# Threshold attention with a GELU layer behind it: early turns split in two, tail copies on another engine, weight conversion shifted between slots

## The chip, the cores and the metric

The kernel runs on one core of one Trainium2 chip. The core has a matrix engine (TensorE, "PE" in the profile, with its weight loads shown apart as "PEld"), a vector engine (VectorE, "DVE"), an activation engine (ScalarE, "ACT"), a general engine (GpSimd, "POOL"), and a queue engine that mostly starts transfers (SyncE, "SP"). They run side by side and wait for each other by semaphores. TensorE writes into PSUM, the small accumulation memory; the others work on SBUF, and VectorE and ScalarE read PSUM too.

The metric is device time in microseconds (us), the median of several runs. Lower is better.

## The reference

```python
scores = scale * np.matmul(q, k.transpose(0, 1, 3, 2))       # q, k, v: (8, 8, 576, 64), float32
thresh = np.max(scores, axis=-1, keepdims=True) - tau
scores = np.where(scores >= thresh, scores, -1000000000.0)
scores = scores - np.max(scores, axis=-1, keepdims=True)
attn = np.exp(scores)
attn = attn / (np.sum(attn, axis=-1, keepdims=True) + 1e-09)
out = np.matmul(attn, v)
x = out.transpose(0, 2, 1, 3).reshape(4608, 512)             # tokens x model
h = x @ w_in                                                 # w_in: (512, 2048)
g = 0.5 * h * (1.0 + erf(h / sqrt(2)))
return g @ w_out                                             # w_out: (2048, 512)
```

Attention per head, in which all keys that score less than the row's best minus tau are dropped, and behind it a two-layer network with an exact GELU. The two weight matrices reach the kernel as 64-bit floating-point numbers; it turns them into 32-bit ones itself.

## The kernel before

**Pairs and slots.** Heads are worked two at a time. There are 32 pairs, four to a batch (HP = 4); the first four (EARLY) are treated differently from the others. The 576 rows of a head are four chunks of 128 (MAIN = 512) and a tail of 64; the two tails of a pair share a fifth chunk. One chunk of one pair is a slot, one turn of the main loop at L1140, counted by `n` from 0. For the early pairs the order is: slots 0 to 7 are chunks 0 and 1 of pairs 0 to 3, slots 8 to 19 are chunks 2, 3 and 4 (the tails) of pairs 0 to 3. From slot 20 (BATCH) on a pair has its five slots in a row. All of the order is written out by hand in this loop; each engine works through its own instructions in the order of the program.

**What a slot does.** `scores` (L403) multiplies the chunk's q with all of k into two PSUM tiles tagged "sc", of which there are two. `softmax_head` takes the negated row maximum on VectorE (L415), the threshold on POOL (L418), and the exponential on ScalarE (L420). `softmax_tail` applies the threshold and sums the row on VectorE (L436); this also frees the "sc" tile for the next slot's scores. Every other PSUM tile has the tag "mm", of which there are four.

**Turning.** For the early pairs q and k are loaded row-wise and transposed by TensorE against the identity, in `turn_qk_early` (L299): 16 matmul records for q, 16 for k, then the tails; one copy of 512 columns for each (L320 for q with its scale, L322 for k, on VectorE for pair zero and on ScalarE for the others), two small copies for k's tail (L330, L331) and two for q's tail (L334). A slot's probabilities are transposed one slot later by `turn_p_early` (L347, nine records) and copied by ScalarE: two copies of 512 columns (L354) and one of 128, the tail columns (L362).

**Weighting.** Two slots after its own, a chunk is multiplied with v. For pairs 2 and 3 (HALVED) this is `weigh_half` for chunk 0 and then for chunk 1 (L606, 128 columns each); for pairs 0 and 1 both chunks together in `weigh_v` (L574, 256 columns), in the slot of the second. `divide_early` then spreads the reciprocals of the row sums over partitions (L493, L495) and POOL multiplies (L501). Chunks 2 to 4 are weighted together later and divided late by `divide_late`; their divisors go through memory on the SP queue (`divisors_early`, L460 to L468).

**Weight conversion.** The weights are 32 pieces (16 of w_in, then 16 of w_out). `load_piece` (L161) starts the transfer of the next raw piece on the SP queue, to one of the seven buffers `xall` or to a part of `turned_p`, and gives up if no buffer is free. A conversion step is two ScalarE activations of 512 columns (`convert_first`, L199, L200), two VectorE operations (`convert_second`, L207, L208), which then ask for another piece, and one POOL addition (L219) in the next slot. `STEPS[n]` says how many steps slot n does, at its end, behind its L436. ScalarE's part runs one piece ahead of VectorE's.

**The network in the early slots.** From slot 10 on `fill` puts the first layer of the first block of tokens between the attention work: some 6.4 matmuls (L674) a slot. Eight matmuls complete a tile hT; it is appended to `late` and copied out of PSUM by ScalarE (L641) when `gelus` is called with a smaller number than are waiting: `lag` inside the fill, 0 after the exponentials of every slot. `keep_busy` adds idle matmuls (L297) in slots 1, 6 and 8.

**Behind slot 20** the same loop goes on with other helpers; `lag` is set to 2 there, and `last_blocks` ends the kernel.

## Time and profile before

| what | value |
|---|---|
| median of 3 runs | 1329.47 us (1329.26 to 1331.39) |
| the profiled execution, its own time | 1329.71 us |
| its span, first to last instruction | 1327.70 us |
| TensorE busy | 1315.7 us, 99% |
| VectorE busy | 1040.3 us, 78% |
| ScalarE busy | 604.9 us, 46% |
| GpSimd busy | 637.1 us, 48% |
| first scores of slot 0 | 7.57 us |
| first scores of slot 10 | 57.21 us |
| first scores of slot 20 | 121.03 us |

The profile is of one execution. Its times count from the first instruction; the execution as timed from outside took 2.01 us more. A matmul of 32-bit numbers shows as two records. The end of a matmul is modelled, so a busy TensorE may hide short waits, for example inside a row of score records that is split in two because the second "sc" tile came free late. In a row of the timeline the brackets at the end give how long the engine stood idle and what it waited for. "In line" below means an operation right behind another on its engine, which starts before the shown end of the one in front of it; what it adds is less than its own duration.

### The profile page before, as it was taken

To read this page: it belongs to the slowest core of one execution; us is meant where nothing else is said; L and a number is where in the kernel's file an instruction comes from. 1 tells how busy PE (TensorE), PEld (TensorE's weight loads), DVE (VectorE), ACT (ScalarE), POOL (GpSimd) and SP (SyncE) were. 2 spreads that over 40 slices of the span, in tenths; PEclk is the share of its full clock that TensorE was granted. 3 is DMA by queue.
4 is the path that set the end of the run, shared out by engine and by line. 5 is a ranking of instruction groups with operands and counts; after the bars stand their busy time and mean duration, and the time that the engine had idled before them with its cause. 6 is when DMAs were issued, how large, how long until landed. Compare 5 with 4: busy or idle time off the path is not lost.

```text
span 1327.7 us, 19863 instructions
## 1 busy us (share of the span) xinstructions
PE 1315.7 (99%) x6306; PEld 889.1 (67%) x6306; DVE 1040.3 (78%) x2001; ACT 604.9 (46%) x1027; POOL 637.1 (48%) x1058
## 2 busy tenths in 40 slices
PE   9999999999999999999999999999999999999998
PEld 6776466576476466466466466578778787877877
DVE  6887877888888888888888888883857698386674
ACT  7988366376376368358458438232111203211120
POOL 3565545455555555655555541236264403645430
PEclk9999999999999999999999999999999999999999
DMA  7553667777776787787787775400000140000003
GB/s 250 180 177 89 143 156 164 168 161 161 190 167 157 191 185 160 191 194 164 185 202 159 177 172 110 105 9 1 1 0 1 40 107 14 0 1 0 1 0 80
DMA packets 213687, 153.14 MB, mean 115 GB/s; under 512 B 117264, under 2 KB 196992, under 8 KB 213584
## 3 DMA queue, kind: packets, MB, share of 16 engines
q1 hardware_dynamic: 195440, 125.31, 40.6%
q0 software_dynamic: 17712, 26.26, 7.4%
q8 instruction: 52, 0.85, 0.3%
q14 instruction: 51, 0.42, 0.1%
q10 hardware_dynamic: 432, 0.30, 0.1%
HBM read 56.62 MB, written 12.58 MB: 52 GB/s over the span
## 4 chain that ended last, share of the span: by engine, by line
PE 92%; ACT 2%; DVE 2%; DMA 1%; issue 1%; POOL 1%; SPq 0%; DVEq 0%; POOLq 0%; ACTq 0%
PE bank L862 34%; PE o_ps L689 17%; PE hT L674 16%; PE sc L403 13%; PE xT L574 11%; ACT p L420 1%; DVE nmx L415 1%; DMA inv<-turned 0%; PE tr L347 0%; ACT pT L354 0%; DVE p L436 0%; DVE power L208 0%; DVE power L207 0%; DMA xall<-in_moe_w_out_dram 0%; DMA turned_p<-in_moe_w_out_dram 0%
## 5 line engine op out<-in xcount | busy, mean ns | idle before, releaser
L420 ACT ACTIVATE p<-sc,nmx 128x576 f32<-128x576 f32 x288 | 202.0, 738 | 277.9 <-DVE nmx L415 277.6
L436 DVE SCALAR_TENSOR_TENSOR p<-sc,thr,p 128x576 f32<-128x576 f32 x288 | 225.4, 816 | 72.7 <-ACT p L420 65.2
L418 POOL TENSOR_SCALAR thr<-nmx,tau_eff 128x1 f32<-128x1 f32 x288 | 84.7, 296 | 335.1 <-DVE nmx L415 332.5
L674 PE MATMUL hT<-xall,w_in 128*128 128x256 f32 x1024 | 241.8, 385 | 0.0
L415 DVE TENSOR_REDUCE nmx<-sc 128x1 f32<-128x576 f32 x288 | 205.2, 749 | 44.3 <-PE sc L403 43.0
L689 PE MATMUL o_ps<-w_out,g 128*128 128x512 f32 x512 | 236.7, 602 | 0.0
L674 PEld LDWEIGHTS hT<-xall,w_in 128*128 128x128 f32 x1024 | 189.4, 190 | 51.3 <-issue 24.5
L744 DVE TENSOR_TENSOR o<-o,bank 128x256 f32<-128x256 f32 (+1 forms) x242 | 100.0, 417 | 94.5 <-PE bank L862 89.5
L744 DVE TENSOR_TENSOR c<-c,bank 128x320 f32<-128x320 f32 x304 | 146.7, 487 | 34.3 <-PE bank L862 21.1
L689 PEld LDWEIGHTS o_ps<-w_out,g 128*128 128x128 f32 x512 | 93.1, 190 | 109.6 <-issue 106.8
L403 PE MATMUL sc<-kT,qT 64*128 64x288 f32 x960 | 161.3, 429 | 2.1 <-DVE p L436 1.2
L574 PE MATMUL xT<-pT,v 128*64 128x320 f32 (+1 forms) x1240 | 159.3, 409 | 0.2
L535 DVE STREAM_TRANSPOSE turned_p<-p 128x1152 f32<-128x1152 f32 x112 | 154.4, 1378 | 3.9
L403 PEld LDWEIGHTS sc<-kT,qT 64*128 64x128 f32 x960 | 91.8, 186 | 77.0 <-issue 61.9
L574 PEld LDWEIGHTS xT<-pT,v 128*64 128x64 f32 x1240 | 86.4, 137 | 70.9 <-issue 10.4
L862 PE MATMUL bank<-w_out,c 128*128 128x256 f32 (+1 forms) x484 | 120.5, 379 | 0.8 <-DVE o L744 0.8
L260 POOL DMA_DIRECT2D v<-in_v_dram x208 | 111.2, 538 | 3.4 <-issue 1.2
L862 PEld LDWEIGHTS bank<-w_out,c 128*128 128x128 f32 x484 | 90.3, 190 | 18.9 <-DVE o L744 3.2
L929 ACT ACTIVATE c<-c 128x320 f32<-128x320 f32 (+1 forms) x80 | 46.9, 624 | 114.7 <-DVE c L744 114.6
L744 POOL TENSOR_TENSOR c<-c,g 128x320 f32<-128x320 f32 (+1 forms) x40 | 50.6, 1273 | 67.4 <-DVE c L744 67.4
L862 PE MATMUL bank<-t_out,g 128*128 128x256 f32 (+1 forms) x324 | 82.4, 377 | 0.4 <-DVE o L744 0.4
L862 PE MATMUL bank<-t_out,c 128*128 128x256 f32 x320 | 82.8, 381 | 0.0
(185 smaller groups left out, 1749.1 us busy)
## 6 DMA issues: line engine op xcount, KB each, us to landing
pT<-turned_p SPq DMA_DIRECT2D x448, 160.0 KB, 3.6
pT<-pd_tail SPq DMA_DIRECT2D x112, 80.0 KB, 3.0
q<-in_q_dram POOLq DMA_DIRECT2D x104, 72.0 KB, 3.6
k<-in_k_dram POOLq DMA_DIRECT2D x104, 72.0 KB, 3.2
inv<-turned SPq DMA_DIRECT2D x54, 128.0 KB, 4.0
v<-in_v_dram POOLq DMA_DIRECT2D x156, 40.0 KB, 3.1
out_dram<-o SPq DMA_DIRECT2D x40, 128.0 KB, 2.4
xall<-in_moe_w_out_dram SPq DMA_DIRECT2D x9, 512.0 KB, 4.9
```

Source lines behind the costliest of these rows:

```text
L260: eng.dma_start(t[r:P:4, e, 0:n, :], rows[:, r * KR:r * KR + n, :])
L403: nc.tensor.matmul(sc[e][:, h, 0:HALF], lhsT=lhsT, rhs=s["kT"][rows, at:at + HALF], start=True, stop=True)
L415: nc.vector.tensor_reduce(nmx[:, e:e + 1], sc, axis=AXIS.XY, op=ALU.max, negate=True)
L418: nc.gpsimd.tensor_scalar(thr[:, e:e + 1], nmx[:, e:e + 1], -1.0, tau_eff, op0=ALU.mult, op1=ALU.subtract)
L420: nc.scalar.activation(w[:, e * S:(e + 1) * S].rearrange("p (h s) -> p h s", h=2), sc, AF.Exp, bias=nmx[:, e:e + 1], scale=1.0)
L436: nc.vector.scalar_tensor_tensor(row, sc[e][:, :, 0:HALF], thr[:, e:e + 1], row, op0=ALU.is_ge, op1=ALU.mult, accum_out=den[e])
L535: nc.vector.transpose(turned_p[:, :, i // 2, 0:NB, i % 2 * Q:(i % 2 + 1) * Q], w.rearrange("p (e b i) -> p e b i", e=2, i=Q))
L574: nc.tensor.matmul(to, lhsT=s["v"][:, e, c, :], rhs=rhs, start=(c == 0), stop=(c == KR - 1))
L674: nc.tensor.matmul(hT[:, j % 2, :], lhsT=w_in_sb[c][:, j * P:(j + 1) * P], rhs=x_blk[n][:, c, :], start=(c == 0), stop=(c == N_DM - 1))
L689: nc.tensor.matmul(o[:, 0:d_model], lhsT=g[j][:, m * P:(m + 1) * P], rhs=w_out_sb[j], start=(j == 0), stop=(j == N_DF - 1))
L744: eng.tensor_tensor(out, a, b, op=ALU.add)
L862: nc.tensor.matmul(to, lhsT=l, rhs=r, start=start and k == 0, stop=k == len(pairs) - 1, skip_group_check=not start)
```

## The change

Six edits, most of them in the early slots:

- `turn_qk_early` takes the names that it turns. Pair one is turned whole in slot 0 as before; of pairs two and three q is turned in the slot where both were, and k one slot later (slots 2 and 3, 4 and 5). For pair zero the order becomes k, tails, q, and q is copied in two halves. The tail of q is written into a tile that is zero elsewhere: two matmuls with a zero operand (`none`) fill the other parts, and one copy of 128 columns replaces the two of 64.
- `turn_p_early` gets a list `later`: for chunks 0 and 1 (slots 1 to 8) the copy of the tail columns moves from ScalarE to VectorE, behind the slot's `softmax_tail`.
- HALVED goes: pairs 0 and 1 are weighted in halves as well.
- STEPS: one step less in slots 6 and 8, one more in slots 16 and 17. The sum stays 32.
- `lag` starts at 0 instead of 1.
- `load_piece` remembers requests that found no free buffer (`wanted`) and serves them at a later call.

```diff
@@ -156,32 +156,33 @@
     LATER = 2
     raws = []
     loaded = [0]
+    wanted = [0]
     converted = [0]
 
     def load_piece(eng=nc.sync):
-        k = loaded[0]
-        if k == len(pieces):
-            return
...
+        wanted[0] += 1
+        while wanted[0] > 0 and loaded[0] < len(pieces):
+            k = loaded[0]
+            staged = k % 2 and k < len(pieces) - LATER
+            if wide and not staged and not x_free:
+                return
+            dst, src = pieces[k]
+            loaded[0] += 1
...
+            wanted[0] -= 1
+            slot = []
+            if staged:
...
@@ -296,11 +297,13 @@
-    def turn_qk_early(p):
+    def turn_qk_early(p, names="qk"):
 
 
         s = st[p]
-        if 2 <= p < HP:
+        if names == "k":
+            qT, kT = s["qT"], s["kT"]
+        elif 2 <= p < HP:
...
@@ -309,32 +312,55 @@
         s["qT"], s["kT"] = qT, kT
         qt = s["q_tail"] = q_tail[p % 4]
         copy = nc.scalar.copy if p else nc.vector.tensor_copy
-        for name in "qk":
-            t = s[name]
+        tiles = {name: s.pop(name) for name in names}
+
+        def most(name, parts=1):
+            t = tiles[name]
             tr = ps.tile([P, NC, P], FP32, tag="mm", name="tr")
-            for c in range(NC):
+            n = NC // parts
+            for part in range(parts):
+                for c in range(part * n, (part + 1) * n):
+                    for e in range(2):
+                        nc.tensor.matmul(tr[e * D:(e + 1) * D, c, :], lhsT=t[:, e, c, :], rhs=ident, start=True, stop=True)
+                src = tr[:, part * n:(part + 1) * n, :].rearrange("p c s -> p (c s)")
+                if name == "q":
+                    nc.scalar.activation(qT[:, part * n * P:(part + 1) * n * P], src, AF.Copy, bias=0.0, scale=q_scale)
+                else:
+                    copy(kT[:, TAIL:S], src)
+
+        def tails():
+            tr = ps.tile([P, NC, P], FP32, tag="mm", name="tr")
+            if "q" in names:
+                none = q_tail[HP - 1][0:TAIL, D:2 * D]
                 for e in range(2):
-                    nc.tensor.matmul(tr[e * D:(e + 1) * D, c, :], lhsT=t[:, e, c, :], rhs=ident, start=True, stop=True)
-            src = tr.rearrange("p c s -> p (c s)")
-            if name == "q":
-                nc.scalar.activation(qT, src, AF.Copy, bias=0.0, scale=q_scale)
-            else:
-                copy(kT[:, TAIL:S], src)
-        tr = ps.tile([P, NC, P], FP32, tag="mm", name="tr")
-        for j, name in enumerate("qk"):
-            t = s.pop(name)
-            for e in range(2):
-                nc.tensor.matmul(tr[e * D:(e + 1) * D, j, 0:TAIL], lhsT=t[0:TAIL, e, NC, :],
-                                 rhs=ident[0:TAIL, 0:TAIL], start=True, stop=True)
-        x_free.extend(s.pop(name + "_slot") for name in "qk" if name + "_slot" in s)
-        nc.scalar.copy(kT[:, S:S + TAIL], tr[:, 1, 0:TAIL])
-        nc.scalar.copy(kT[D:P, 0:TAIL], tr[D:P, 1, 0:TAIL])
-        for e in range(2):
-            rows = slice(e * D, (e + 1) * D)
-            nc.scalar.activation(
-                qt[rows, e * TAIL:(e + 1) * TAIL], tr[rows, 0, 0:TAIL], AF.Copy, bias=0.0, scale=q_scale[rows])
-
-    def turn_p_early(p, i):
+                    nc.tensor.matmul(tr[e * D:(e + 1) * D, 0, (1 - e) * TAIL:(2 - e) * TAIL], lhsT=ident[0:TAIL, 0:D],
+                                     rhs=none, start=True, stop=True)
+            for j, name in enumerate(names):
+                for e in range(2):
+                    at = e * TAIL if name == "q" else 0
+                    nc.tensor.matmul(tr[e * D:(e + 1) * D, j, at:at + TAIL], lhsT=tiles[name][0:TAIL, e, NC, :],
+                                     rhs=ident[0:TAIL, 0:TAIL], start=True, stop=True)
+            if "k" in names:
+                nc.scalar.copy(kT[:, S:S + TAIL], tr[:, j, 0:TAIL])
+                nc.scalar.copy(kT[D:P, 0:TAIL], tr[D:P, j, 0:TAIL])
+            if "q" in names:
+                yield
+                nc.scalar.activation(qt, tr[:, 0, :], AF.Copy, bias=0.0, scale=q_scale)
+
+        if p == 0:
+            most("k")
+            rest = tails()
+            next(rest)
+            most("q", 2)
+            next(rest, None)
+            return
+        for name in names:
+            most(name)
+        for _ in tails():
+            pass
+        x_free.extend(s.pop(name + "_slot") for name in names if name + "_slot" in s)
+
+    def turn_p_early(p, i, later=None):
 
...
@@ -359,7 +385,10 @@
         tr = ps.tile([P, NC, P], FP32, tag="mm", name="tr")
         turn(tr[:, 0, :], MAIN if i < NC else S - P)
         if i < NC:
-            nc.scalar.copy(tails[:, i * P:(i + 1) * P], tr[:, 0, :])
+            if later is None:
+                nc.scalar.copy(tails[:, i * P:(i + 1) * P], tr[:, 0, :])
+            else:
+                later.append(lambda: nc.vector.tensor_copy(tails[:, i * P:(i + 1) * P], tr[:, 0, :]))
...
@@ -626,7 +655,7 @@
     BLK_NS = N_DF * (N_DM * NS_IN + TOK // P * NS_OUT)
 
     late = []
-    lag = [1]
+    lag = [0]
...
@@ -1127,14 +1156,14 @@
 
     PARTS = 1.3, 1.3, 0.2, 1.3, 0.9
 
-    HALVED = (2, 3)
     DIVIDE_LATE = {14: 0, 16: 1, 19: 2, 22: 3}
-    STEPS = [0, 1, 1, 1, 1, 1, 2, 1, 2, 2, 2, 2, 3, 2, 2, 3, 2, 2, 1, 0, 1]
+    STEPS = [0, 1, 1, 1, 1, 1, 1, 1, 1, 2, 2, 2, 3, 2, 2, 3, 3, 3, 1, 0, 1]
     BUSY = {1: 2, 6: 2, 8: 2}
 
     tokens = 0
     owed = 0.0
     due = []
+    later = []
...
@@ -1149,8 +1178,10 @@
                 invert(*last)
             if last and last[0] < EARLY and last[1] == NC:
                 divisors_early(last[0])
-            if p < HP - 1 and i == 0:
-                turn_qk_early(p + 1)
+            if p == 0 and i == 0:
+                turn_qk_early(1)
+            elif p < HP - 1 and i < 2 and n > 1:
+                turn_qk_early(p + 1, "qk"[i])
         elif n == len(slots):
...
@@ -1169,8 +1200,6 @@
                 xT = weigh_v(*args, None)
                 continue
             weigh_v(*args)
-            if args[1] == 0:
-                divide_early(*args)
         due = []
...
         if last and last[0] < EARLY and last[1] < NC:
-            turn_p_early(*last)
+            turn_p_early(*last, later if last[1] < 2 else None)
         if p < NP:
             softmax_tail(p, i)
+        while later:
+            later.pop(0)()
         if n == BATCH - 1:
...
         if last and last[0] < EARLY:
-            if last[1] < 2 and last[0] in HALVED:
-                due.append((last[0], last[1]))
-            elif last[1] == 1:
-                due.append((last[0], 0, TOK))
+            if last[1] < 2:
+                due.append(last)
             if last[1] == NC and early:
                 due.append((last[0], TOK, S))
```

More of the change, by code (lines that the diff above doesn't have):

```diff
@@ L158 @@
     loaded = [0]
+    wanted = [0]
     converted = [0]
     def load_piece(eng=nc.sync):
-        k = loaded[0]
-        if k == len(pieces):
-            return
-        staged = k % 2 and k < len(pieces) - LATER
-        if wide and not staged and not x_free:
-            return
-        dst, src = pieces[k]
-        loaded[0] += 1
-        if not wide:
-            nc.sync.dma_start(dst, src)
-            converted[0] += 1
-            load_piece()
-            return
-        slot = []
-        if staged:
-            half, at = divmod(k // 2 % 4, 2)
-            raw = pd[half].bitcast(U32)[:, at * 2 * PIECE:(at + 1) * 2 * PIECE]
-        else:
-            slot = [x_slot()]
-            raw = x_rows(slot[0]).bitcast(U32)
-        eng.dma_start(raw, src.bitcast(U32))
-        raws.append((dst, raw, slot))
+        wanted[0] += 1
[6 more added lines that the diff above has]
+            loaded[0] += 1
+            if not wide:
+                nc.sync.dma_start(dst, src)
+                converted[0] += 1
+                continue
+            wanted[0] -= 1
+            slot = []
+            if staged:
+                half, at = divmod(k // 2 % 4, 2)
+                raw = pd[half].bitcast(U32)[:, at * 2 * PIECE:(at + 1) * 2 * PIECE]
+            else:
+                slot = [x_slot()]
+                raw = x_rows(slot[0]).bitcast(U32)
+            eng.dma_start(raw, src.bitcast(U32))
+            raws.append((dst, raw, slot))
     ahead = []
@@ L311, in turn_qk_early @@
         copy = nc.scalar.copy if p else nc.vector.tensor_copy
-        for name in "qk":
-            t = s[name]
+        tiles = {name: s.pop(name) for name in names}
+        def most(name, parts=1):
+            t = tiles[name]
             tr = ps.tile([P, NC, P], FP32, tag="mm", name="tr")
-            for c in range(NC):
-                for e in range(2):
-                    nc.tensor.matmul(tr[e * D:(e + 1) * D, c, :], lhsT=t[:, e, c, :], rhs=ident, start=True, stop=True)
-            src = tr.rearrange("p c s -> p (c s)")
-            if name == "q":
-                nc.scalar.activation(qT, src, AF.Copy, bias=0.0, scale=q_scale)
-            else:
-                copy(kT[:, TAIL:S], src)
@@ L361, in turn_p_early @@
         if i < NC:
-            nc.scalar.copy(tails[:, i * P:(i + 1) * P], tr[:, 0, :])
+            if later is None:
+                nc.scalar.copy(tails[:, i * P:(i + 1) * P], tr[:, 0, :])
+            else:
+                later.append(lambda: nc.vector.tensor_copy(tails[:, i * P:(i + 1) * P], tr[:, 0, :]))
             return
```

## The prediction

> **What bounds the kernel now.** "Slot n" is turn n of the main loop (numbered from 0). I read the page first, then the table of busy time over stretches that I cut at the slots' first score matmuls (slots 0 and 1; 2 to 5; 6 to 9; 10 to 15; 16 and 17; 18 and 19; the rest), then the chain of waits, then the timeline of the first 121 us.
>
> ```profile
> PE 1315.7 (99%) x6306; PEld 889.1 (67%) x6306; DVE 1040.3 (78%) x2001; ACT 604.9 (46%) x1027; POOL 637.1 (48%) x1058
> ```
> ```profile
> 7.57:15.58 8.01, 7.50 (x74) 5.79 (x74) 5.45 (x12) 5.84 (x14) 1.44 (x5) 1.00 0.92 293
> 15.58:37.73 22.15, 21.56 (x205) 15.22 (x205) 17.43 (x39) 21.27 (x47) 9.82 (x18) 1.00 0.82 271
> 37.73:57.21 19.48, 18.61 (x182) 14.06 (x181) 18.09 (x38) 18.05 (x39) 10.98 (x19) 1.00 0.49 157
> 96.36:106.67 10.31, 10.01 (x55) 7.83 (x53) 8.65 (x16) 8.44 (x18) 9.08 (x11) 1.00 0.52 170
> 121.03:1327.70 1206.67, 1200.56 (x5469) 803.95 (x5468) 943.90 (x1796) 503.30 (x818) 573.28 (x957) 1.00 0.47 108
> ```
>
> Columns: stretch, length, then busy PE, PEld, DVE, ACT, POOL. After 121.03 us TensorE is 99.5% busy on work that the diff leaves alone, so whatever the first 20 slots gain or lose moves the end by as much. In slots 2 to 5 ScalarE is fuller (96%) than anywhere else, but TensorE shows 97% too. In 6 to 9 VectorE and ScalarE tie at 93%.
>
> The chain of waits around slots 2 and 3:
>
> ```profile
> 7.35 0.22 ACT kT L331
> 7.57 1.22 PE sc L403 x7
> ...
> 20.15 0.58 ACT qT L320
> 20.73 0.48 ACT pd_tail L322
> ...
> 22.20 0.60 ACT pT L354
> 22.80 0.04 issue
> 22.84 2.54 PE xT L574 x19
> ```
>
> ScalarE's turn copies for pair two hold it from 20.15 to 22.84; then TensorE alone carries it to 28.49.
>
> The timeline, at three places that decide: the start, the boundary of slots 8 and 9, and slots 16 and 17.
>
> ```profile
> 6.62 0.20 PEld L327 LDWEIGHTS tr<-ident,q 64*64 64x64 f32 x4 [0.17 <-DMA q<-in_q_dram]
> 6.74 0.69 DVE L322 COPY kT<-tr 128x512 f32<-128x512 f32 x1
> ```
> ```profile
> 53.91 0.69 DVE L208 SCALAR_TENSOR_TENSOR power<-turned_p,power 128x512 uint32<-128x512 uint32 x1
> 54.52 1.41 DVE L415 TENSOR_REDUCE nmx<-sc 128x1 f32<-128x576 f32 x2
> ```
> ```profile
> 100.52 1.64 DVE L208 SCALAR_TENSOR_TENSOR power<-xall,power 128x512 uint32<-128x512 uint32 x1
> 102.44 0.61 DVE L207 TENSOR_SCALAR power<-power 128x512 uint32<-128x512 uint32 x1 [0.27 <-ACT power L199]
> 103.08 0.70 DVE L208 SCALAR_TENSOR_TENSOR power<-turned_p,power 128x512 uint32<-128x512 uint32 x1
> 103.70 1.41 DVE L415 TENSOR_REDUCE nmx<-sc 128x1 f32<-128x576 f32 x2
> ```
>
> First: the tail of pair zero's q lands at about 6.6 and holds TensorE. Second and third: the row maximum of a slot starts the moment that the last conversion of the slot before it ends, so a conversion step there is on the path.
>
> **What the Trainium skill says.** "PSUM — Partial Sum Buffer", Engine vs sequencer instructions: ScalarE, VectorE and GpSimd queues are strict FIFO. The pairs of rows above agree (54.52 right behind 53.91). "GPSIMD Engine Reference", Specifications: its SBUF interfaces are shared with VectorE, with contention when a VectorE instruction has two SBUF inputs. L208 has two; its durations are 0.69 least and median, 1.64 most, and the long ones at 81.60 and 100.52 run beside two POOL additions of L219. "VectorE: DVE Perf Modes", The TRN2 errata, is used below for a price.
>
> **The change part by part.** The sum is against the profiled execution: 1329.71 us, a span of 1327.70 with 2.01 around it; it lies 0.24 above the median of 1329.47.
>
> *Pair zero.* Now: q, k, tails; the first scores at 7.57 wait for the k tail copies (7.12, 7.35), which follow the q tail that lands at 6.6. After: k (done near 5.3 instead of 6.7), then the tails, then q in halves. The big k copy gains nothing: on VectorE it stands behind eight memsets that end at 6.74. The tails still wait for the landing at 6.6 and end near 7.05. Only then do q's first 8 records run, some 0.6 (16 take 1.09), to about 7.65; their 128x256 copy takes 0.38 (row of L495, ScalarE), so scores start near 8.15: **+0.58**. If the landing were as quick as the main parts (about 3 us, 4.8 us at 1.8 + 3), they would start at about 7.7: +0.1; if scores wait for both halves, +1.0. I take 0.58. Slots 0 and 1 are a closed ring of score, maximum, exp, mask, with nothing to win.
>
> *ScalarE in slots 1 to 9.* Removed: eight tail copies (0.28 alone, 0.16 in line), 8 x 0.16 = 1.3; for pairs two and three, two 0.31 activations become one of 128x128 (nearest L362, 0.17 in line), 2 x 0.45 = 0.9; one conversion step each from slots 6 and 8, two activations of 0.57 in line each, 2 x 1.14 = 2.3. The k turns of pairs two and three (0.48 + 0.11 + 0.21) go one slot later, to slots 3 and 5. Their inputs' release moves with them; pieces loaded into those buffers don't wait, as they are asked for behind the turn. Block 0 gets its buffer in slot 2, behind q's turn.
>
> *TensorE in slots 2 to 5.* Pairs zero and one are now weighted in halves: 2 x 1.24 (38.90 to 40.14) for 2.54. Two zeroing matmuls per q (4 records, some 0.2 with a gap). For two slots: scores 2 x 1.17, turns 2.28 + 0.32, halves 2.48, divisors 0.65, turned p 2 x 1.14: 10.35. Slots 4 and 5 take 10.53 now, so hardly 0 to 0.2 is left there; slots 2 and 3 take 11.62, with 0.7 of a split score in the first. By following the four PSUM buffers through slots 2 and 3, I get 11.3. So the 2.2 us that ScalarE sheds here find TensorE behind them: **-0.33**.
>
> *VectorE in slots 1 to 8.* Eight copies of 128x128 out of PSUM, behind the masks. The named errata table gives 120 + 128 cycles at 0.96 GHz, 0.26, an estimate; the trace has no such copy but 0.21 for 128x64 and 0.39 for 128x256 (127.0 us), which agrees. Behind each stand a conversion and the next maximum: 0.26 a slot where VectorE binds (slots 6 to 8). There one step of L207 and L208 (0.42 + 0.69 = 1.11) leaves slots 6 and 8. Chained through: slot 7's maximum 44.25 becomes 43.65; slot 8 starts 0.55 sooner, slot 9 only 0.35, since two rounds of idle matmuls stand ahead of its scores; slot 9's maximum 54.52 becomes 53.45. Slot 10 starts **0.86** sooner.
>
> *Layer-one copies (lag 0).* The eight hT copies (0.49 in line) keep their number and go ahead of the pT copies of the same slot. The third transpose of a slot now waits for the first pT copy (0.29, 0.24, 0.24, 0.30, 0.30 in slots 12, 13, 16, 17, 18) because two hT tiles hold PSUM; it will not. What is late next in 14 and 15 is the mask on VectorE (0.27 at 87.53). I take **-0.4** for 12 and 13, **-0.4** for 18 and 19, and nothing in 16 and 17, where VectorE binds. Ends: 0 to -1.4.
>
> *Slots 16 and 17, a step more each.* In 16: after 100.52 and 103.08 a third pair follows; its ScalarE half is done at 103.42, so the maximum of 103.70 comes at about 104.85. **+0.95** with the 0.2 that the lost transpose wait gives. The step in 17 delays slot 18's maximum from 109.95 to 112.3; its mask then ends at 115.6 instead of 113.25, while the scores of slot 19 come at 115.45 plus 1: covered by TensorE's 7.7 us of weighting, layer one and transposes in slot 18. Without that cover it is 1.11 more.
>
> *Loads on SP.* Each step asks for one piece, so from piece 14 on loads come one or two slots later, conversions too, seven in flight throughout. SP is closed from 67.27 to 79.10 by divisors and eight loads for pair four; what stands behind is needed in slot 14 either way. Pieces 27 to 30 now come behind the next divisors (97.96, landing 4.6 later at 102.6), and are read near 104. The remembered request applies to piece 31 only, in slot 15, which is loaded one slot later and needed in 18: nothing.
>
> Sum: +0.58 - 0.33 - 0.86 - 0.4 + 0.95 - 0.4 = -0.46: 1329.25 in the profiled execution, **1329.0** for the median.
>
> **The rivals.** *ScalarE alone binds slots 1 to 9.* Then all 4.5 of it come off, with 1.4 of transpose waits, against 0.58 and 0.95: -4.4, 1325.1. For it: 96% busy, and the chain from 20.15. Against: TensorE's own 10.35 per two slots. *Slots 16 and 17 pay in full.* Three L219 additions per slot on POOL meet L207 and L208; a step then costs 0.61 + 1.64 = 2.25, and slot 18's cover is used up: 2 x 2.25 for 0.95 gives +3.1, 1332.6. For it: both long L208 are in such slots. Against: 18's cover. It decides from about 4.1 us in those two steps. *The early slots were never full*, so that only start and late steps count: +0.58 + 0.95 - 0.4, 1330.6, inside no change.
>
> **How the numbers follow.** 0.2% is 2.7 us, about what a measurement of this kernel can tell from no change. My forecast with its own range (1327.3 to 1331.0) and the third rival: 0.62. ScalarE bound, in whole or in most: 0.22. Late slots in full: 0.16. The two outer cases reach 1325.1 and 1332.6; the range stops just inside them, 1325.4 to 1332.2.
>
> **What would show it.** First scores near 8.15, not 7.57; slot 2's start some 0.6 later; slots 2 to 5 near 21.8 with ScalarE below 90%; slot 10 some 0.6 sooner than 57.21; no wait of the third transpose for pT in slots 12 and 13; slot 17 a microsecond longer; slot 20 near 120.6 for 121.03. Wrong if a load is late in slots 16 and 17, if slots 2 to 5 shrink below 21, or if the 1206.67 us behind slot 20 change.

## The result, and the profile after

The changed kernel took 1327.78 us (median of 22 runs, 1326.33 to 1330.93), the kernel before 1330.22 us on the same chip (22 runs, 1329.13 to 1332.19). The ratio is 0.9984, with a 95% interval from 0.9978 to 0.9989: about 0.16% faster, 2.1 us (2.4 by the medians). That is inside the 0.2% that the prediction calls no change, but the interval lies wholly below one: with 22 runs the change can be told from none. The profiled execution took 1327.03 us with a span of 1325.30, against 1329.71 and 1327.70 before.

The page's first line of the changed kernel, which answers the one shown of before:

```profile
PE 1313.4 (99%) x6362; PEld 890.3 (67%) x6362; DVE 1042.8 (79%) x2009; ACT 601.9 (45%) x1018; POOL 634.2 (48%) x1058
```

The table of stretches of the changed kernel, cut at the same slots (columns as before: stretch, length, busy PE, PEld, DVE, ACT, POOL, granted clock, share of the DMA engines, GB/s):

```profile
8.71:16.74 8.03, 7.58 (x80) 5.78 (x78) 5.45 (x12) 5.69 (x13) 1.42 (x5) 1.00 0.93 308
16.74:37.97 21.23, 21.21 (x252) 16.45 (x253) 17.77 (x42) 19.89 (x43) 9.24 (x18) 1.00 0.84 279
37.97:55.92 17.95, 17.75 (x182) 14.08 (x181) 16.46 (x38) 14.99 (x31) 9.59 (x17) 1.00 0.32 99
55.92:94.12 38.20, 36.99 (x207) 27.56 (x205) 33.51 (x67) 34.10 (x70) 21.83 (x29) 1.00 0.58 184
94.12:105.57 11.45, 9.64 (x55) 7.82 (x53) 9.81 (x18) 10.14 (x20) 8.50 (x11) 1.00 0.70 245
105.57:119.47 13.90, 13.75 (x79) 10.06 (x79) 12.29 (x23) 12.19 (x26) 9.01 (x13) 1.00 0.40 72
119.47:1325.30 1205.83, 1199.62 (x5469) 803.62 (x5468) 944.80 (x1797) 502.54 (x818) 571.45 (x957) 1.00 0.47 108
```

Two rows of the kernel before that the prediction did not show:

```profile
57.21:96.36 39.15, 37.72 (x206) 27.68 (x205) 34.04 (x67) 34.37 (x69) 22.90 (x30) 1.00 0.58 182
106.67:121.03 14.36, 13.93 (x80) 10.10 (x79) 9.86 (x21) 11.04 (x25) 6.49 (x11) 1.00 0.40 74
```

The two tables side by side give the whole account of the profiled execution:

| part | before | after | difference | forecast |
|---|---|---|---|---|
| first scores of slot 0 | 7.57 | 8.71 | +1.14 | +0.58 |
| slots 0 and 1 | 8.01 | 8.03 | +0.02 | 0 |
| slots 2 to 5 | 22.15 | 21.23 | -0.92 | -0.33 |
| slots 6 to 9 | 19.48 | 17.95 | -1.53 | -0.86 |
| slots 10 to 15 | 39.15 | 38.20 | -0.95 | -0.4 |
| slots 16 and 17 | 10.31 | 11.45 | +1.14 | +0.95 |
| slots 18 and 19 | 14.36 | 13.90 | -0.46 | -0.4 |
| behind slot 20's scores | 1206.67 | 1205.83 | -0.84 | 0 |
| span | 1327.70 | 1325.30 | -2.40 | -0.46 |

From slot 0 to slot 20, which is where the change acts, 113.46 us became 110.76: -2.70 where the forecast's terms give -1.04. The first row varies between executions whatever the code, and of the last only 0.38 repeats, as the experiments show. The rows between them repeat to some 0.05 us in kernels with the same code there (slots 16 and 17 to 0.3), so single profiles can be compared by them.

In slots 2 to 5 TensorE is busy for 21.21 of 21.23 us; the chain of waits names nothing else there. One row, the scores of slot 2, takes 1.95 instead of 1.24; no other is longer than its fellows. At the start it names a copy that the prediction did not have:

```profile
6.96 0.61 PE tr L324 x8
...
7.59 0.48 ACT qT L327
...
8.12 0.66 PE tr L324 x8
8.78 1.22 PE sc L432 x8
```

The second half of pair zero's q is transposed only when ScalarE has copied the first half out of the same PSUM tile. In slots 16 and 17, the timeline of the changed kernel shows the third step:

```profile
97.95 1.51 DVE L208 TENSOR_SCALAR power<-power 128x512 uint32<-128x512 uint32 x1
99.49 1.11 DVE L209 SCALAR_TENSOR_TENSOR power<-xall,power 128x512 uint32<-128x512 uint32 x1
...
101.71 0.42 DVE L208 TENSOR_SCALAR power<-power 128x512 uint32<-128x512 uint32 x1
102.17 0.69 DVE L209 SCALAR_TENSOR_TENSOR power<-xall,power 128x512 uint32<-128x512 uint32 x1
102.77 1.42 DVE L444 TENSOR_REDUCE nmx<-sc 128x1 f32<-128x576 f32 x2
```
```profile
105.57 1.94 PE L432 MATMUL sc<-pd_tail,qT 64*128 64x288 f32 x8 [1.81 <-DVE p L465]
```

These are the first and the third step of slot 16. The maximum of slot 17 starts 8.65 us behind the scores of slot 16 (102.77 - 94.12); before it was 7.34 (103.70 - 96.36). TensorE then stands idle for 1.81 us ahead of slot 18's scores. (L208 and L209 of the changed kernel are L207 and L208 of the kernel before.)

### The profile page after: what moved, and what is told of

It is laid out like the page before. It is cut to its first block, busy times and chain, and to the rows that moved or that the text cites. A ratio compares the mean times of both kernels' runs of the same rounds, so it can differ in the third digit from the quotient of the medians.

```text
span 1325.3 us, 19980 instructions
## 1 busy us (share of the span) xinstructions
PE 1313.4 (99%) x6362; PEld 890.3 (67%) x6362; DVE 1042.8 (79%) x2009; ACT 601.9 (45%) x1018; POOL 634.2 (48%) x1058
## 4 chain that ended last, share of the span: by engine, by line
PE 93%; DVE 2%; issue 1%; DMA 1%; ACT 1%; POOL 1%; SPq 0%; POOLq 0%; DVEq 0%; ACTq 0%
PE bank L891 34%; PE o_ps L718 17%; PE hT L703 16%; PE sc L432 13%; PE xT L603 11%; PE tr L373 1%; DVE nmx L444 1%; PE xT L635 1%; PE tr L324 1%; DVE power L209 1%; DVE power L208 0%; ACT p L449 0%; DVE p L465 0%; DMA inv<-turned 0%; DMA turned_p<-in_moe_w_out_dram 0%
## 5 line engine op out<-in xcount | busy, mean ns | idle before, releaser
L603 PE MATMUL xT<-pT,v 128*64 128x320 f32 (+1 forms) x1200 | 153.6, 410 | 0.0
L603 PEld LDWEIGHTS xT<-pT,v 128*64 128x64 f32 x1200 | 83.4, 137 | 68.0 <-issue 10.4
```

The costliest lines, as they stand in the source:

```text
L603: nc.tensor.matmul(to, lhsT=s["v"][:, e, c, :], rhs=rhs, start=(c == 0), stop=(c == KR - 1))
```

## The experiments

The two theories at the outset: the one of the prediction, in which TensorE carries slots 2 to 5, VectorE carries slots 6 to 9 and the late steps cost about one microsecond; and the rival that ScalarE alone held the early slots. To tell the parts apart, three kernels do one part alone (e3, e4, e7), four undo or alter one part of the changed kernel (e1, e2, e10, e12), and three go on from the result (e8, e9, e11). All the work of the kernel stays in each (e9 leaves out idle matmuls). This table has their profiled executions in us, cut at each kernel's own first scores; each line is one execution. "20 to 30" is from slot 20's scores to slot 30's, a part of "behind 20".

| kernel | slot 0 at | 2 to 5 | 6 to 9 | 10 to 15 | 16, 17 | 18, 19 | slot 0 to 20 | 20 to 30 | behind 20 |
|---|---|---|---|---|---|---|---|---|---|
| before | 7.57 | 22.15 | 19.48 | 39.15 | 10.31 | 14.36 | 113.46 | 55.75 | 1206.67 |
| after | 8.71 | 21.23 | 17.95 | 38.20 | 11.45 | 13.90 | 110.76 | 55.37 | 1205.83 |
| e1 | 8.23 | 21.23 | 17.94 | 38.17 | 11.19 | 13.91 | 110.44 | 55.36 | 1209.83 |
| e2 | 8.19 | 21.24 | 17.96 | 38.18 | 11.46 | 15.29 | 112.17 | 55.38 | 1206.54 |
| e3 | 8.41 | 22.18 | 17.82 | 38.72 | 11.39 | 14.71 | 112.83 | 56.13 | 1206.26 |
| e4 | 8.78 | 22.13 | 19.47 | 38.62 | 10.17 | 13.60 | 112.00 | 55.36 | 1206.52 |
| e7 | 8.60 | 21.24 | 20.15 | 39.15 | 10.31 | 14.36 | 113.21 | 55.75 | 1208.19 |
| e10 | 8.70 | 21.39 | 17.80 | 38.17 | 11.21 | 13.90 | 110.51 | 55.37 | 1206.59 |
| e12 | 9.03 | 21.22 | 17.95 | 38.18 | 12.47 | 12.92 | 110.78 | 55.38 | 1205.89 |
| e8 | 7.59 | 21.23 | 17.95 | 38.20 | 10.20 | 13.60 | 109.18 | 55.84 | 1205.83 |
| e9 | 7.29 | 21.23 | 17.81 | 37.99 | 10.16 | 13.59 | 108.78 | 55.85 | 1206.03 |
| e11 | 8.00 | 21.22 | 17.96 | 38.75 | 10.31 | 14.36 | 110.60 | 56.00 | 1208.20 |

### The start: pair zero's order (e1, e2)

e1 is the changed kernel with pair zero turned in the old order:

```diff
-        if p == 0:
-            most("k")
-            rest = tails()
-            next(rest)
-            most("q", 2)
-            next(rest, None)
-            return
```

> The changed kernel with pair zero turned in the old order (q whole, k, tails), the one q-tail copy and the zeroing matmuls kept. Theory: the new order alone costs the 1.14 us by which slot 0's first scores came later (8.71 for 7.57), and slots 0 and 1 hand it on whole. Then slot 0 starts at 7.6 to 7.8, slot 10 at 54.8 to 55.0 (55.92 in the changed kernel), slot 20 near 118.4 and the time is about 1.1 us below the changed kernel's. Rival: slots 2 to 5 have slack that takes up a late start; then slot 10 stays within 0.3 of 55.92 and the time does not move.

It took 1328.36 us (1326.1 to 1331.67, 10 runs), ratio to the kernel before 0.9983 (0.9972 to 0.9994): no gain over the changed kernel. Slot 0 started at 8.23, not at 7.6 to 7.8.

e2 keeps the new order, but gives each half of q a PSUM tile of its own:

```diff
-            tr = ps.tile([P, NC, P], FP32, tag="mm", name="tr")
             n = NC // parts
             for part in range(parts):
+                tr = ps.tile([P, NC, P], FP32, tag="mm", name="tr")
```

> The changed kernel with one more PSUM tile: the two halves of pair zero's q are turned into two tiles instead of one. Theory: 0.55 of the late start is TensorE's wait for ScalarE's copy of the first half before it may write the second half into the same tile (0.57 idle at 8.12); with two tiles slot 0 starts at 8.1 to 8.2, which is the forecast's number. Rival: the scores wait for both halves' copies in any case; then they start at 8.5 or later.

One execution, 1328.67 us. The timeline of e2 at the start, TensorE's rows:

```profile
6.96 1.09 PE L324 MATMUL tr<-ident,q 128*64 128x128 f32 x16
8.19 1.00 PE L432 MATMUL sc<-kT,qT 64*128 64x288 f32 x6
```

and the changed kernel's row at the same place:

```profile
8.12 0.66 PE L324 MATMUL tr<-ident,q 128*64 128x128 f32 x8 [0.57 <-ACT qT L327]
```

(Its slots 18 and 19 took 15.29 for another reason, told at the end.) With two tiles both halves run in one go and the scores come at 8.19, close to the 8.15 of the prediction; the wait of 0.57 was the shared tile. The Trainium skill, "PSUM — Partial Sum Buffer", PSUM bank collisions raise a hardware error, says that two engines are to be kept apart by PSUM bank and block of 32 partitions, not by address; this wait of 0.57, for a copy of other columns of the same tile, agrees.

What the order is worth can't be read from 7.57 and 8.71 alone. The old order started slot 0 at 7.57, 8.41, 8.78, 8.23, 8.60, 7.59, 7.29 and 8.00 in eight kernels; the new order on one tile at 8.71, 8.70 and 9.03. The traces show where the 1.5 us of the old order's spread come from. In all of them TensorE starts its first transposes of pair zero at 4.16 or 4.17, and in the old order the scores come 0.94 to 1.14 behind the first weight load for the tails. What differs is how fast TensorE gets through the 32 records between. The row of k's, first in the kernel before, then in e4, which has the same code here:

```profile
5.64 1.06 PE L317 MATMUL tr<-ident,k 128*64 128x128 f32 x15
```
```profile
6.14 1.76 PE L317 MATMUL tr<-ident,k 128*64 128x128 f32 x15
```

No row of TensorE's in e4 between 4.16 and 7.83 names a transfer that it waits for (in e1 and e11 one does, for 0.20 and 0.31). The clock record of the traces starts, with full clock, at 4.26, 4.50, 5.10, 5.62, 6.20, 6.65, 7.07 and 7.41 us in e9, e8, before, e11, e1, e3, e7 and e4; slot 0 starts at 7.29, 7.59, 7.57, 8.00, 8.23, 8.41, 8.60 and 8.78. The order is the same but for one pair 0.02 apart. (What stood ahead of it is not recorded.) So the start goes with the moment from which TensorE has full clock, and kernels are to be compared in which that moment is alike:

| full clock from | old order | new order, one tile | later by |
|---|---|---|---|
| 6.20 (e1), 6.18 (e10) | 8.23 | 8.70 | 0.47 |
| 6.65 (e3), 6.62 (after) | 8.41 | 8.71 | 0.30 |
| 7.07 (e7), 7.15 (e12) | 8.60 | 9.03 | 0.43 |

By these three pairs the new order costs 0.3 to 0.5 us. In the one pair there is, two tiles don't bring it ahead of the old one either: e2, with full clock from 4.91, starts at 8.19, the kernel before, from 5.10, at 7.57.

### One part alone (e3, e4, e7)

e3 is the kernel before with the new STEPS:

```diff
-    STEPS = [0, 1, 1, 1, 1, 1, 2, 1, 2, 2, 2, 2, 3, 2, 2, 3, 2, 2, 1, 0, 1]
+    STEPS = [0, 1, 1, 1, 1, 1, 1, 1, 1, 2, 2, 2, 3, 2, 2, 3, 3, 3, 1, 0, 1]
```

> The kernel before with the new STEPS alone. Theory (the forecast's parts): slots 6 to 9 shrink by about 0.9 (slot 10 starts at 56.3 for 57.21), slots 16 and 17 grow by 1.0 to 1.2 (10.31 to about 11.4), slot 20 stays within 0.4 of 121.03 and the time within 0.5 us. Rival, ScalarE binds the early slots: slots 2 to 9 shrink by the whole 2.3 us of the two steps, slot 10 starts at 55.0 or sooner and slot 20 at 120 or sooner. Rival, late steps paid in full: slots 16 to 19 grow by 3 us or more.

It took 1330.17 us (1328.62 to 1331.34, 12 runs), ratio 0.9997 (0.9988 to 1.0005): nothing. The table of stretches of e3 shows why:

```profile
38.60:56.42 17.82, 17.75 (x182) 14.09 (x181) 15.99 (x34) 15.65 (x35) 9.19 (x17) 1.00 0.38 118
...
95.14:106.53 11.39, 10.02 (x55) 7.84 (x53) 9.75 (x18) 9.63 (x20) 9.40 (x11) 1.00 0.70 246
106.53:121.24 14.71, 14.11 (x80) 10.02 (x80) 12.33 (x23) 12.16 (x26) 8.84 (x13) 1.00 0.41 72
```

Slots 6 to 9 gain 1.66 and 10 to 15 another 0.43; slots 16 and 17 lose 1.08, and slots 18 and 19 lose 0.35. Of 2.1 gained, 1.4 is given back, and another 0.38 between slots 20 and 30 (56.13 for 55.75). None of TensorE's three waits for a ScalarE copy that stood in slots 7 to 9 of the kernel before (shown further down) is left in e3.

e4 is the kernel before with the layer-one copies sooner:

```diff
-    lag = [1]
+    lag = [0]
```

> The kernel before with lag 0 alone. Theory: nothing until slot 11, then the waits of a slot's third transpose for the first pT copy go in slots 12, 13, 16, 17 and 18 (0.24 to 0.30 each) and slot 20 starts 0.8 to 1.4 sooner than 121.03. Rival: VectorE's masks (0.27 and 0.48 of idle at 87.53 and 68.26) take the gain back; then slot 20 stays within 0.3 of 121.03.

One execution, 1329.31 us. Nothing moves up to slot 10; then slots 10 to 15 gain 0.53, slots 16 and 17 0.14, slots 18 and 19 0.76, in all 1.46 from slot 0 to slot 20, and 0.39 more up to slot 30. Slots 12 and 13 alone gain 0.97; slot 14 gives 0.43 back, as VectorE's mask is late next (TensorE waits 0.69 for it ahead of slot 15, 0.27 before). The waits that go are those that the prediction named. TensorE in slot 12, first the kernel before, then e4:

```profile
76.10 1.04 PE L347 MATMUL tr<-ident,p 128*128 128x128 f32 x8
77.43 0.33 PE L347 MATMUL tr<-ident,p 128*128 128x128 f32 x1 [0.29 <-ACT pT L354]
```
```profile
77.30 1.15 PE L347 MATMUL tr<-ident,p 128*128 128x128 f32 x9
```

e7 is the changed kernel with STEPS, lag and pair zero's order as before, so that the split turns, the tail copies on VectorE and the weighting in halves stand alone:

```diff
-        if p == 0:
-            most("k")
...
-    lag = [0]
+    lag = [1]
...
-    STEPS = [0, 1, 1, 1, 1, 1, 1, 1, 1, 2, 2, 2, 3, 2, 2, 3, 3, 3, 1, 0, 1]
+    STEPS = [0, 1, 1, 1, 1, 1, 2, 1, 2, 2, 2, 2, 3, 2, 2, 3, 2, 2, 1, 0, 1]
```

> The changed kernel with pair zero's old order, the old STEPS and lag 1: only the split turns, the one q-tail copy, the tail copies on VectorE and the halves for all pairs are left of the change. Theory: TensorE bounds slots 2 to 5, so these take 21.2 us (22.15 before), and slots 6 to 9 stay at 19.3 to 19.8 (19.48 before), as VectorE with two steps in slots 6 and 8 binds there. Slot 20 comes at 112.3 to 112.8 from slot 0 (113.46 before). Rival, ScalarE binds slots 6 to 9 too: they fall to 18.5 or less.

One execution, 1331.73 us; behind slot 20 it took 1208.19, 1.5 more than the kernel before. Slots 2 to 5 take 21.24, all of the gain that they have in the changed kernel. But slots 6 to 9 take 20.15, longer than the 19.48 of the kernel before. The stretch of e7:

```profile
37.84:57.99 20.15, 18.60 (x182) 14.06 (x181) 18.58 (x42) 17.35 (x35) 11.38 (x19) 1.00 0.47 152
```

ScalarE lost 0.7 us of work there (18.05 to 17.35) and VectorE gained 0.5 (18.09 to 18.58), and the slots became 0.67 longer: VectorE held them, and four tail copies of 0.29 stand in its row. e7 doesn't tell the split turns, the one q-tail copy and the halves apart; for the tail copies e10 does. From slot 0 to slot 20 the three parts give -0.63, -1.46 and -0.25, together -2.34, where the changed kernel has -2.70 and e1, without pair zero's order, -3.02. So they hardly overlap, and a little is gained by having them together.

### The tail copies (e10)

e10 is the changed kernel with the copies of the tail columns left on ScalarE:

```diff
-            turn_p_early(*last, later if last[1] < 2 else None)
+            turn_p_early(*last)
```

> The changed kernel with the eight tail copies back on ScalarE. Theory: they were off the path on ScalarE, and on VectorE they cost 0.26 only where VectorE binds. So slots 2 to 5 stay at 21.2 to 21.5, slots 6 to 9 at 17.7 to 18.0 (17.95 in the changed kernel), slot 20 within 0.3 of the changed kernel's 110.76 from slot 0. Rival, ScalarE's load sets slots 2 to 5: they grow by 0.6 us or more.

One execution, 1327.66 us. Slots 2 to 5 lose 0.16, slots 6 to 9 gain 0.15, slots 16 and 17 gain 0.24. From slot 0 to slot 20 it is 110.51 against 110.76, but the 0.24 is no more than what slots 16 and 17 vary by (11.19 in e1, 11.45 and 11.46 in the changed kernel and e2): with the steps moved, this edit is worth nothing that shows.

### The late steps and the idle stretch ahead of slot 18 (e8, e12)

e8 takes e1 and puts the two steps into slots 18 and 19 instead of 16 and 17:

```diff
-    STEPS = [0, 1, 1, 1, 1, 1, 1, 1, 1, 2, 2, 2, 3, 2, 2, 3, 3, 3, 1, 0, 1]
+    STEPS = [0, 1, 1, 1, 1, 1, 1, 1, 1, 2, 2, 2, 3, 2, 2, 3, 2, 2, 2, 1, 1]
```

> The changed kernel with pair zero's old order and the two late conversion steps in slots 18 and 19 instead of 16 and 17. Times are given from slot 0's first scores, since these start where the first loads land. Theory: the step in slot 16 costs about 1.1 us and TensorE's idle stretch of 1.8 us ahead of slot 18's scores; in slots 18 and 19 a step is hidden behind TensorE's weighting and layer one. So slots 16 and 17 fall from 11.2 or more to about 10.1, slot 20 comes at 109.0 to 109.5 from slot 0 (110.44 with the steps in 16 and 17), and the median lies 1.0 to 1.5 us below the changed kernel's, some 3.5 to 4 us below the kernel before. Rival: the steps only move their cost along, to slots 18 to 20; then slot 20 stays at 110.2 or later.

(What is on record for e9 and e11 says "slots 18 and 20" of e8; the steps stand in slots 18 and 19.) It took 1325.76 us (1324.37 to 1332.88, 15 runs) beside 1330.61 for the kernel before, ratio 0.9973 (0.9964 to 0.9983). That is below the kernel before. By medians, which were taken on different occasions, it is 2.0 us below the changed kernel; the two intervals overlap. From slot 0 to slot 20 it is 109.18, 1.26 less than e1, from which it differs in this alone. Its stretches from slot 16 on:

```profile
92.97:103.17 10.20, 9.64 (x54) 7.80 (x53) 8.60 (x16) 8.78 (x19) 8.60 (x11) 1.00 0.64 227
103.17:116.77 13.60, 13.58 (x80) 10.11 (x80) 11.58 (x24) 11.68 (x25) 7.71 (x12) 1.00 0.49 104
```

In slots 18 and 19 TensorE is busy for 13.58 of 13.60 us; the two steps lie beside it and cost nothing there. 10.20 and 13.60 are what e4 has with no late step at all (10.17 and 13.60). But the rival holds in part: some of the cost moves on behind slot 20, where the table's cut hides it. Slot 21's scores come 4.47 behind those of slot 20 for 4.04 in e1, and TensorE waits for the mask:

```profile
121.24 1.94 PE L425 MATMUL sc<-kT,qT 64*128 64x288 f32 x8 [0.39 <-DVE p L458]
```

Up to slot 30 that makes 55.84 for 55.36. The two steps cost 0.5 us in this place, and e8's gain over e1 is 0.8 and not 1.26.

e12 is the changed kernel with idle matmuls at the end of slot 17, meant to fill TensorE's idle 1.8 us:

```diff
-    BUSY = {1: 2, 6: 2, 8: 2}
+    BUSY = {1: 2, 6: 2, 8: 2, 17: 2}
```

> The changed kernel with two rounds of idle matmuls (eight records, 1.1 us) more, at the end of slot 17, where TensorE idles for 1.8 us. Theory: in some executions that idle stretch makes the granted clock fall in slot 18 (in the two-tile kernel 0.87 from 100 to 110 us, slot 18 took 10.1 us instead of 8.4); the filler stands in idle time and costs nothing itself. Then the marks up to slot 18 stay within 0.2 of the changed kernel's, slot 18 takes 8.4, and the runs that lie over 1.5 us above the lowest become fewer than the changed kernel's 9 of 22. Rival: the lower clock comes from elsewhere; then the spread of the runs stays as it is, and slot 18's scores come later by what the filler takes.

It took 1329.37 us (1326.51 to 1335.62, 21 runs), ratio 0.9992 (0.9984 to 1.0000). The filler did not fill the idle stretch. It waits in its turn for a copy of ScalarE's, for 1.74 us, and pushes slot 18's scores back:

```profile
105.81 1.16 PE L298 MATMUL idle<-ident 128*128 128x128 f32 x8 [1.74 <-ACT g L670]
```

Slot 18 starts a microsecond later, slots 18 and 19 are that much shorter, and slot 0 to slot 20 stays at 110.78. The runs scatter more and not less: 14 of 21 lie over 1.5 us above the lowest, of the changed kernel's 22 it is 11 (the expectation has 9). But as the idle stretch stayed, e12 says nothing about its theory. e8 says more: with 0.56 us of idle ahead of slot 18, four of its 15 runs are still over 4 us above its lowest.

### What binds slots 6 to 9 now (e9), and the copies again (e11)

e9 is e8 without the idle matmuls of slots 6 and 8:

```diff
-    BUSY = {1: 2, 6: 2, 8: 2}
+    BUSY = {1: 2}
```

> The changed kernel with pair zero in its old order, the two late conversion steps in slots 18 and 20 (as in e8), and without the idle matmuls of slots 6 and 8. In e8 TensorE is busy 17.75 us of the 17.95 us of slots 6 to 9, and 2.3 us of that are these idle matmuls. Theory: after the change TensorE is what binds there, so without them slots 6 to 9 shrink until VectorE's 16.46 us hold them: 16.5 to 17.2, slot 0 to slot 20 at 107.9 to 108.5 instead of 109.2, and the time 0.7 to 1.3 us below that of e8. Rival one: the ring of maximum, exponential and mask holds the slots and TensorE only looks full, so nothing moves: 17.8 to 18.0, time as e8. Rival two: with TensorE less busy its granted clock falls in slots 6 to 9 or 10 to 15 (below 0.98 in the table of stretches), and the slots behind grow by a microsecond or more.

It took 1325.37 us (1323.85 to 1325.67, 5 runs), ratio 0.9963 (0.9949 to 0.9977). Against e8's interval (0.9964 to 0.9983) that is no difference; e9 beats the kernel before. It just clears the changed kernel's interval too (0.9978 to 0.9989), from five runs and without the two side by side. The stretch of slots 6 to 9, first of e8, then of e9:

```profile
36.82:54.77 17.95, 17.75 (x182) 14.09 (x182) 16.46 (x38) 14.98 (x31) 9.60 (x17) 1.00 0.43 143
```
```profile
36.52:54.33 17.81, 17.00 (x165) 12.74 (x165) 16.31 (x38) 15.17 (x31) 9.85 (x18) 1.00 0.48 160
```

The theory asked for 16.5 to 17.2 and fell; the first rival holds. Sixteen idle records (2.3 us) fewer shorten the slots by 0.14. Without the idle matmuls slot 9 starts 13.22 behind slot 6 instead of 14.06, but slot 10 only 0.14 sooner. Nor was TensorE's 17.75 all work: a row of scores whose second "sc" tile is late shows its wait as busy time, as here in e9:

```profile
40.66 1.95 PE L425 MATMUL sc<-pd_tail,qT 64*128 64x288 f32 x8 [0.52 <-DVE p L458]
```

The same eight records take 1.24 where nothing is late. The ring of scores, maximum, exponential and mask over TensorE, VectorE and ScalarE holds these slots, with VectorE busy for 16.3 of the 17.8 us.

e11 is e8 with `lag` back at 1 (the diff of e4 turned round).

> The kernel of e8 (changed kernel, pair zero in its old order, the two late conversion steps in slots 18 and 20) with lag back at 1. Theory: the layer-one copies that go sooner are worth in the changed kernel what they were worth in the old one, about 0.5 in slots 10 to 15, 0.15 in slots 16 and 17 and 0.8 in slots 18 and 19: 38.6 to 38.8, 10.2 to 10.5 and 14.0 to 14.6, slot 0 to slot 20 at 110.3 to 110.8 instead of 109.18. Rival: with the steps moved, ScalarE has room in these slots and the later copies cost nothing: within 0.3 of 109.18. In slots 2 to 9 nothing changes under either (21.23 and 17.95).

One execution, 1328.57 us, 2.4 of it behind slot 20 against e8. 38.75, 10.31 and 14.36 are inside or at the figures of the theory; slot 0 to slot 20 is 110.60 for e8's 109.18. The sooner copies are worth 1.42 in the changed kernel and 1.46 in the old one (up to slot 30: 1.58 and 1.85).

## Why the prediction was right or wrong

The case that came true is the forecast's own, between 1327.3 and 1331.0, but near its lower end: -0.46 was forecast for the profiled execution, and -2.40 came. That it stayed in this case is owed to the width of the range as much as to the sum, for the terms were not off at random. Three of them, slots 2 to 5, 6 to 9 and 10 to 15, brought about twice what was forecast, all to the same side. The signs of all terms hold. Of the rivals, none came true as a whole; VectorE operations stretched beside GpSimd's additions, on which the second rests, are there (1.51 and 1.11 for one step at 97.95), but they were there before the change too, and its 3.1 us did not come.

**Pair zero's order, +0.58.** The sign is right, and like for like the order costs 0.3 to 0.5. The step "scores start near 8.15" left out that both halves of q share a tile: the wait of 0.57, which e2 takes away. The copy took 0.47 and not 0.38, too. Without the shared tile the working comes out: e2 starts at 8.19, 0.62 later than the kernel before, with full clock from nearly the same moment. One reading is not borne out, that the landing of q's tail at 6.6 holds TensorE: the 0.17 us ahead of the tails, for which the profile of before names this load, stand there in all eight kernels with the old order, and mostly no load is named. What moves the start is the time of the 32 transposes, of which the prediction said nothing; it moves single executions by up to 1.5 us.

**Slots 2 to 5, -0.33.** The bound was right: TensorE is behind the relieved ScalarE, busy for 21.21 of 21.23 us, and the rival's 4.5 us did not come. The size was not: -0.92. The step that failed is "By following the four PSUM buffers through slots 2 and 3, I get 11.3": it took 11.01 (16.74 to 27.75), and slots 4 and 5 took 10.22 where 10.35 was added up and 10.53 stood before. The plain sum, twice 10.35 and the 0.7 of a split score, gives 21.4; following the buffers by hand put 0.4 on top of it and was worse. e7 gives this term alone, 21.24. Putting the tail copies back costs 0.16 of it (e10); how the rest divides between the split turns, the one q-tail copy and the halves is not separated.

**Slots 6 to 9, -0.86.** It was -1.53. That VectorE binds there was right; the chain that was followed through it broke off too soon, and the failed step is "slot 9 only 0.35, since two rounds of idle matmuls stand ahead of its scores". Measured from slot 6, slot 8 came 0.33 sooner, slot 9 0.86 and slot 10 1.53. The idle matmuls do hold slot 9's start (e9), but before the change they had themselves to wait for VectorE, by way of ScalarE. The chain of waits of the kernel before in slot 8 (L207 and L208 are a conversion step, L415 the maximum, L420 the exponential, L608 the copy of the weighted chunk):

```profile
47.63 0.89 DVE power L207
48.55 0.69 DVE power L208
49.24 0.68 DVE nmx L415
49.94 1.41 ACT p L420 x2
51.34 0.17 ACT xall L608
```

The chain goes on with TensorE's idle matmuls at 51.56 and the scores of slot 9. TensorE in slots 7 to 9 of the kernel before waited three times for this copy:

```profile
46.65 0.33 PE L347 MATMUL tr<-ident,p 128*128 128x128 f32 x1 [0.20 <-ACT xall L608]
...
51.56 1.16 PE L297 MATMUL idle<-ident 128*128 128x128 f32 x8 [0.26 <-ACT xall L608]
...
56.93 0.33 PE L347 MATMUL tr<-ident,p 128*128 128x128 f32 x1 [0.34 <-ACT xall L608]
```

In the changed kernel none of these three waits is left, and none in e3, which moves only the steps. It is VectorE's half of the steps that counts: ahead of these exponentials ScalarE itself stood idle for the maximum (0.25, 0.75 and 0.37 us). In e7, where ScalarE has less to do and VectorE more, the same three waits are 0.55, 0.26 and 0.53, together longer by more than half. Besides, L207 took 0.96 at 47.55 before and takes 0.42 now, so a slot lost more than the 1.11 that the two operations take at their best. VectorE's busy time agrees: 2 x 1.11 for two steps and 0.54 for that L207 go, four tail copies of 0.29 come, -1.6; the table has 18.09 and 16.46. The tail copies were priced well (0.26, measured 0.29), and so was where they count: e7 shows them as a loss where two steps stand beside them.

**The copies of layer one, -0.4 and -0.4.** The first: right, -0.53 in e4 (0.97 won in slots 12 and 13, 0.43 lost in slot 14). Another 0.43 in slots 10 to 15 comes from the moved steps (e3), a term that the prediction did not have: of it 0.1 falls in slot 10 and 0.33 in slot 11. Slots 18 and 19: -0.46 came for -0.4, but out of two others: the copies give -0.76 (e4), and the late step takes 0.35 (e3), which the prediction had as covered.

**Slots 16 and 17, +0.95.** Right, +1.14. VectorE binds there, the maximum of slot 17 came 1.31 later for the 1.15 forecast, and the rival's 4.1 us in two steps did not come. That steps there are a cost was an argument that led further than the prediction took it: the same two steps in slots 18 and 19, under TensorE's work, cost less by 0.8 us (e8).

**ScalarE's relief, and what it is worth.** The rival of a bound ScalarE is refuted by e7: with the 2.2 us of copies gone from ScalarE that the prediction counted (1.3 and 0.9), slots 2 to 5 gain only the 0.9 that TensorE's own work allows, and slots 6 to 9 lose 0.67.

**Not touched: behind slot 20.** The prediction put nothing here and named a change of the 1206.67 as a sign of being wrong. 1206.67 became 1205.83. Of these 0.84, 0.38 fall between slots 20 and 30 and belong to the change: e4 has them from `lag` alone (55.36 for 55.75), e7, without it, has none. The remaining 0.46 are not assigned; kernels with the same code there show 1205.8 to 1209.8.

## What to carry to other kernels

When work is taken off an engine, follow the wait to its end: here three waits of TensorE for a ScalarE copy, 0.8 us in all, were VectorE's lateness handed on, and went with its work. Where work has to go somewhere, look for slots in which another engine is full from end to end: two steps cost 1.3 us more under a row maximum on VectorE than beside a full TensorE, though 0.5 of that turned up again behind slot 20. So cut the table well behind the last slot that an edit touches. At the start of a kernel compare only executions in which the clock was alike. A full TensorE in the profile is a bound only if its records are work: rows that are longer than their fellows hold waits, and taking idle matmuls out of a stretch that looked 99% full gained 0.14 us.

## What the runs showed that was not expected

**TensorE's clock after a short idle time.** In e2, as in the changed kernel, TensorE stood idle ahead of slot 18, for 1.82 and 1.81 us. The changed kernel went on at full clock. e2 did not; its table of stretches from 106 us on (the clock is the third number from the end):

```profile
106.00:108.00 2.00, 2.00 (x12) 1.11 (x12) 1.97 (x3) 2.00 (x4) 1.03 (x2) 0.83 0.10 23
108.00:110.00 2.00, 2.00 (x10) 0.86 (x8) 1.93 (x5) 2.00 (x4) 0.00 (x0) 0.50 0.49 94
110.00:112.00 2.00, 2.00 (x12) 0.99 (x9) 1.61 (x4) 1.29 (x3) 1.69 (x3) 0.82 0.56 91
```

0.83, 0.50 and 0.82 in three stretches of 2 us make 0.68 + 2 + 0.72 = 3.4 us at half clock, which loses 1.7 us; slot 18 took 10.09 us in e2 and 8.39 in the changed kernel, just that. The Trainium skill, "TensorE: Matmul & The Clock Gate", Part 1, says that the clock is halved after an idle window of about 3.4 us and given back after a busy one, and that the windows run freely, so that the effect varies from run to run. The 3.4 us at half clock agree, and so does that one of two nearly equal stretches is hit; but the idle time ahead of it was 1.82 us, well short of such a window.

This is also how the runs scatter. The nine of the changed kernel's 22 runs with a mean granted clock (a share of full speed) of 0.999 or more took 1326.33 to 1327.56 us, the thirteen with 0.997 or 0.998 took 1327.63 to 1330.93. In e1, e8 and e12 the same line parts the runs without an overlap (in e3 it does not). The nine have a median of 1327.02, all 22 one of 1327.78. A stretch of 3.4 us at half clock takes 0.0013 off the mean of 1325 us and adds 1.7 us. Of the kernel before, 64 of 65 runs beside the experiments have 0.999 or more. So the changed kernel loses part of its gain to the clock. Which of its idle times bring this about stays open: the profiles caught two, this one and the stall of e1 told next.

**A late transfer in the middle of the kernel.** e1, e2, e7 and e11 have a stall of TensorE near 684 us, of 2.51, 0.78, 1.24 and 0.73; e8 has none at this place. In e1, in the timeline:

```profile
678.73 1.69 POOL L644 TENSOR_TENSOR xall<-xall,inv 128x128 f32<-128x128 f32 x3 [2.98 <-DMA inv<-turned]
680.36 2.16 POOL L261 DMA_DIRECT2D v<-in_v_dram  x4
```
```profile
682.90 0.82 DVE L458 SCALAR_TENSOR_TENSOR p<-sc,thr,p 128x576 f32<-128x576 f32 x1 [3.70 <-POOL thr L440]
```

The divisors' transfer had been issued by 671.63 and was waited for until 678.73; GpSimd waited, then started four loads, and only then came the threshold of the next slot, for which VectorE stood still. In e8 the same wait was 0.21 us, in the kernel before 0.60. Behind e1's stall, too, the clock fell (0.86, 0.50 and 0.78 in the stretches of 2 us from 684 on, again 3.4 us at half clock). The stall's 2.5 and the clock's 1.7 are about the 4.0 by which e1's 1209.83 behind slot 20 exceeds the 1205.83 of the changed kernel. Where the late transfer comes from stays open.

**The other VectorE operation suffers too.** The prediction had GpSimd's additions lengthen L208 of before, which has two inputs. In the changed kernel its neighbour with one input took up to 1.74 us where its median is 0.42, at 97.95 and at 106.07, both times beside two additions on GpSimd (2.50 us from 96.67 and from 104.78), about until these were done. The Trainium skill, "GPSIMD Engine Reference", Specifications, gives two cases for such contention, two inputs or a two-port mode of VectorE; whether this operation runs in that mode, no run shows.
